# Where VectorE's sums stand in their slots, and seven products for every pair of token tiles from the fourth on

## The chip, the cores and the metric

The kernel runs on one core of a Trainium2 chip. The metric is the device time of one execution in microseconds (us); of the kernel before, 12 runs are at hand. One further execution was profiled, and all durations below are from it. The engines are called PE (TensorE's matmuls), PEld (its weight loads), DVE (VectorE), ACT (ScalarE), POOL (GpSimd) and SP (SyncE, which issues DMAs).

## What is computed

Attention with a sliding window of 128 and a bias that falls linearly with distance, for 8 batches of 576 tokens and 8 heads of 64, and behind it a two-layer block on all 4608 tokens:

```python
scores = scale * q @ k.T                       # per batch and head
mask = (rel >= 0) & (rel < 128)                # rel = query position - key position
attn = softmax(where(mask, scores - slope * |rel|, -1e9))
x = (attn @ v), heads side by side             # 4608 x 512
h = x @ w_in                                   # 4608 x 2048
g = where(h > 0, h, exp(min(h, 0)) - 1)        # ELU
out = g @ w_out                                # 4608 x 512, float32
```

## The kernel before, in words

The kernel's order is written out by hand. Its unit of order is the **slot**: slots 0 to 151, and most of them hold one *hidden step*, PE's work for one PSUM bank of h, 128 x 512. Tokens are cut into nine tiles t of 512, and for the output into 18 **pairs** n of 256 tokens (two tiles of 128 rows each). What a slot issues is set by lists that are filled beforehand and walked at L646 to L659, in this order: `early` (exponentials of attention scores), the hidden step (`hidden`, L292), the ELU's last operation of the step before (`done`, L523), `tasks` in the order in which they were entered, `OUT` (output matmuls), and `late`. Each engine works strictly through its own instructions in that order, so a place in the list is a place in every engine's queue.

**Hidden step and ELU.** PE fills one of the two banks hp[0] and hp[1] (L300), in turn. Then there are two ways. In a slot that the set SOFT names, ACT does a relu (L307) and an exponential (L308). In any other, ACT does one exponential (L310) and POOL a min and max (L311). Either way DVE follows with one scalar_tensor_tensor (L318) in the next slot, which writes g and frees the bank, so the hidden step two slots on waits for it.

**Attention.** For batches 2 to 7 each batch takes 17 slots from START[b] (L587), in four units of four slots. In a unit's first slot PE computes scores at the end (L225), into four banks. In its second and third slot ACT takes the exponentials (L231, four a unit, two at the head of each slot), and DVE multiplies by a table (`weigh`, L236, two a unit). In its fourth slot PE multiplies by v (`all_values`, L266), DVE divides (L271, L272: a reciprocal and a product, "the norm"), and SP turns the result into xT by a DMA. A short fifth step ends the batch (L248, L254, L255). DVE also turns q and k of a later batch (`turn_qk`, L145).

**Output.** Pairs outside the list SEVEN (L511), which are 0, 1, 2, 6 and 10, use plain products: 32 matmuls of 512 columns, four a slot (L324), and two copies by ACT (L331). The other 13 pairs use seven products in place of eight (Strassen's scheme in Winograd's form): 56 matmuls of 256 columns, seven a slot (L388), over eight slots from s = 15 + 8n. They need four sums of halves of g by DVE, S1 to S4 (`sums`, L358, each 128 x 1024 in float16), three sums of results, C11, C12, C22 (`combine`, L395, each 128 x 256 in float32), five copies by ACT (L391, L393), and differences of w_out that are made once, in eight halves, in slots 26 to 39 (`quarters`, L351). Call p = (s - 15) mod 8 the phase of a slot. S1 of a pair is made in the slot before its first (p = 7), S2 at p = 1, S3 at p = 3, S4 at p = 4. C11 is in `late` at p = 2, C12 in `late` at p = 6, C22 in the tasks of p = 0 of the next pair. The product that needs S2 begins with the third matmul of p = 2. The banks op and av change roles after each pair of SEVEN (XY, L513).

Because the attention tasks are entered into the lists first (L591 to L617), the sums of a slot stand behind its weights, norms and turns in DVE's queue.

Of the kernel before, what the change touches and what calls it, by code (L numbers as in the profile page):

```python
# [18 lines left out]
def kernel(  # L19
# [14 lines left out]
    NTB = NTOK // 512  # L34
# [114 lines left out]
    with tc.manual_schedule():  # L149
# [142 lines left out]
        def hidden(t, c0, w, f0, nf, p, soft):  # L292
            hps[t, c0, f0] = p
            a = (512 * t + c0) % RING
            cuts = [(0, w, a)] if a + w <= RING else [(0, RING - a, a), (RING - a, w, 0)]
            for l in range(nf):
                fc = f0 + l
                for u0, u1, x0 in cuts:
                    for c in range(4):
                        nc.tensor.matmul(  # L300
                            p[:, l * w + u0:l * w + u1], w_in_sb[:, c, fc * 128:(fc + 1) * 128],
                            xT[:, c, x0:x0 + u1 - u0], start=(c == 0), stop=(c == 3))
            e = es[t, c0, f0] = work.tile([128, 512], F32, name="e", tag="e", bufs=6)
            n = w * nf
            if soft:

                nc.scalar.activation(e[:, 0:n], p[:, 0:n], AF.Relu, scale=-1.0)  # L307
                nc.scalar.activation(e[:, 0:n], e[:, 0:n], AF.Exp, scale=-1.0)  # L308
                return
            nc.scalar.activation(e[:, 0:n], p[:, 0:n], AF.Exp)  # L310
            nc.gpsimd.tensor_scalar(out=e[:, 0:n], in0=e[:, 0:n], scalar1=1.0, scalar2=0.0,  # L311
                                    op0=ALU.min, op1=ALU.max)
# [173 lines left out]
        early, tasks, late, HID, OUT = {}, {}, {}, {}, {}  # L486

        def at(s, f, *a):
            tasks.setdefault(s, []).append((f, a))

        def after(s, f, *a):
            late.setdefault(s, []).append((f, a))

# [13 lines left out]
        for t in range(2, NTB):  # L507
            for j in range(16):
                step = (128 * (j // 4), 128, 4 * (j % 4), 4) if t < 4 else (256 * (j // 8), 256, 2 * (j % 8), 2)
                HID[16 * t + 6 + j] = [(t, *step, BUF[(j + 1) % 2])]  # L510
        SEVEN = (17, 3, 4, 5, 7, 8, 9, 11, 12, 13, 14, 15, 16)  # L511

        XY = {1: (op, av)}  # L513
        for n in range(2, 2 * NTB):
            XY[n] = XY[n - 1][::-1] if n - 1 in SEVEN else XY[n - 1]
        for o in range(16 * NTB):
            t, ts, f = o // 16, o // 4 % 4, o % 4
            if o // 8 in SEVEN:
                continue
            s = (9, 11, 13, 14)[o] if o < 4 else 11 + o if o < 13 else 2 * o - 1 if o < 16 else 15 + o  # L520
# [70 lines left out]
        for b in range(2, B):  # L591
            for u in range(4):
                a = START[b] + 4 * u
                after(a, scores, b, u)
                for g in range(4):
                    before(a + 1 + g // 2, expo, b, u, g)
                at(a + 1, weigh, b, u, 0)
                at(a + 2, weigh, b, u, 1)
                at(a + 3, all_values, b, u)
                at(a + 3, turn, b, u)  # L600
                if u == 3:
                    at(a + 4, values, b, 4, 0, sp[2])
                    at(a + 4, values, b, 4, 1, sp[3])
                    at(a + 4, turn, b, 4)
            a = START[b - 1] if b > 2 else 0
            for n in range(4):
                piece = (b, int(n < 2), n % 2)
                if b == 2:
                    m = 4 if n < 2 else 6
                    at(TURN[b][n], turn_qk, *piece, 0, m)  # L610
                    at(REST[n], turn_qk, *piece, m, R)
                else:
                    at(TURN[b][n] if b == 3 else a + 4 * n, turn_qk, *piece)
            for n in range(8):
                at(a - 8 + n if a else 16 + n // 2, load_qk, b, int(n < 4), n % 4)
            for n in range(5):
                at(a + 3 + n if a else 20 + n // 2, load_v, b, n)  # L617


        for m, a in enumerate((26, 30, 31, 32, 34, 35, 36, 39)):  # L620
            at(a, quarters, 1 + m // 2, m % 2)
        turns = [(i, j) for i in (1, 2, 6, 5, 7, 3, 4) for j in range(8)]
        for n in SEVEN:
            s = 15 + 8 * n
            if n < 2 * NTB - 1:
                for d, i in ((-1, 1), (1, 2), (3, 3), (4, 4)):
                    at(s + d, sums, n, i)
                after(s + 2, combine, n, "C11")
                after(s + 6, combine, n, "C12")
                at(s + 8, combine, n, "C22")  # L630
                for d in range(8):
                    OUT[s + d] = [(product, (n, i, j, j + 1)) for i, j in turns[7 * d:7 * d + 7]]
            else:
                at(s - 3, sums, n, 3)
                for i in (1, 2):
                    at(s - 2, sums, n, i, 0, 6)
                    at(s - 1, sums, n, i, 6, 8)
                at(s - 1, product, n, 1)
                OUT[s] = [(product, (n, 2)), (combine, (n, "C11")), (sums, (n, 4)), (product, (n, 6)), (product, (n, 5))]
                OUT[s + 1] = [(product, (n, 7)), (product, (n, 3)), (combine, (n, "C12")), (combine, (n, "C22")),  # L640
                              (product, (n, 4)), (last_out, (n,))]


        SOFT = {15 + 8 * n + d for n in SEVEN for d in (-1, 1, 2, 3, 4)} | {26, 30, 31, 32, 34, 35, 36, 39} | set(range(16 * NTB - 10, 16 * NTB + 8))

        slots = set(HID) | set(OUT) | set(tasks) | set(early)  # L646
        for s in range(min(slots), max(slots) + 1):
            for f, a in early.get(s, []):
                f(*a)
            for step in HID.get(s, []):  # L650
                hidden(*step, s in SOFT)
            if s - 1 in HID and s not in (1, 4, 5):
# [37 lines left out]
```

## Time and profile before

| | |
|---|---|
| median of 12 runs | 314.06 us (313.53 to 316.18) |
| the profiled execution's own time | 314.49 us |
| its span, first to last instruction | 312.7 us |
| PE busy | 303.3 us, 97% |
| PEld busy | 248.6 us, 79% |
| DVE busy | 246.2 us, 79%, 470 instructions |
| ACT busy | 226.4 us, 72%, 432 instructions |
| POOL busy | 123.3 us, 39%, 189 instructions |
| granted TensorE clock | 0.998 |

Busy time counts an instruction from its start to its end. On DVE and ACT a following instruction may start before the one ahead has ended (a scalar_tensor_tensor lasts 0.68 us, but the next starts 0.60 us after it), so the distance from start to start is what an instruction takes of its engine. PE's recorded ends are modelled, and its matmuls overlap. A lost moment of PE shows best as a gap in the weight loads or as a distance between starts that is longer than usual.

### The profile page before, as it was taken

Reading aid. Unit: us, or ns where it says so; the run is one execution under the profiler, and the core shown is the slowest. Engines: PE = TensorE matmul, PEld = TensorE weight load, DVE = VectorE, ACT = ScalarE, POOL = GpSimd, SP = SyncE. Lnnn points to the kernel's source line nnn. Section 1 sums busy time; section 2 is a strip of 40 time slices with the busy share of each in tenths; the row PEclk is TensorE's granted clock in tenths of the full one; section 3 lists DMA queues with packets and bytes.
Section 4 is the critical chain, followed back from the end, with each engine's and each line's share of the span. In section 5 each row is a group of like instructions: output and inputs, shape, how many; then the busy total and the mean of one; then the engine's idle time right before and its main releaser. Section 6 shows DMA issues by size and latency. Waiting matters only on the chain.

```text
span 312.7 us, 10087 instructions
## 1 busy us (share of the span) xinstructions
PE 303.3 (97%) x4231; PEld 248.6 (79%) x4231; DVE 246.2 (79%) x470; ACT 226.4 (72%) x432; POOL 123.3 (39%) x189
## 2 busy tenths in 40 slices
PE   6899999999999999999999999999999999999995
PEld 5688874786798888987788888777899778888884
DVE  5646656889889988886889898778898888886782
ACT  4576457688888677756887779647977787868871
POOL 8847879463333235263716071655210101010000
PEclk9999999999999999999999999999999999999999
DMA  9999999996893919898979999997921201130102
GB/s 97 179 198 201 201 179 151 148 114 68 84 147 67 143 17 146 62 163 93 101 62 141 106 108 73 159 128 64 92 79 27 78 19 55 48 94 1 69 36 101
DMA packets 96510, 32.05 MB, mean 102 GB/s; under 512 B 83920, under 2 KB 91984, under 8 KB 96464
## 3 DMA queue, kind: packets, MB, share of 16 engines
q0 software_dynamic: 75920, 18.36, 65.3%
q1 hardware_dynamic: 20400, 12.98, 18.0%
q8 instruction: 33, 0.54, 0.7%
q14 instruction: 13, 0.11, 0.1%
q10 hardware_dynamic: 144, 0.07, 0.1%
HBM read 36.70 MB, written 9.44 MB: 148 GB/s over the span
## 4 chain that ended last, share of the span: by engine, by line
PE 82%; DVE 6%; ACT 4%; issue 3%; DMA 2%; POOL 1%; DVEq 0%; POOLq 0%; ACTq 0%
PE hp L300 35%; PE op L388 10%; PE av L388 9%; PE op L324 6%; PE spa L225 4%; PE av L324 3%; ACT EX L231 3%; PE spa L266 3%; DVE g L318 2%; DMA s<-in_q_dram 2%; PE sp L388 1%; PE sp L248 1%; PE sp L324 1%; PE sp L300 1%; PE spa L176 1%
## 5 line engine op out<-in xcount | busy, mean ns | idle before, releaser
L300 PE MATMUL hp<-xT,wi 128*128 128x128 f16 (+2 forms) x1744 | 144.9, 233 | 2.1 <-DVE rden L254 0.6
L300 PEld LDWEIGHTS <-wi 128*128 128x128 f16 x1856 | 124.4, 98 | 22.4 <-issue 7.4
L318 DVE SCALAR_TENSOR_TENSOR g<-e,hp 128x512 f16<-128x512 f32 x138 | 94.1, 682 | 23.6 <-POOL e L311 16.2
L311 POOL TENSOR_SCALAR e<-e 128x512 f32<-128x512 f32 x70 | 43.9, 627 | 149.4 <-ACT e L310 148.7
L307 ACT ACTIVATE e<-hp 128x512 f32<-128x512 f32 x74 | 44.3, 599 | 25.1 <-PE hp L300 22.0
L310 ACT ACTIVATE e<-hp 128x512 f32<-128x512 f32 x64 | 38.5, 602 | 27.0 <-PE hp L300 24.5
L308 ACT ACTIVATE e<-e 128x512 f32<-128x512 f32 x74 | 46.7, 631 | 2.4
L236 DVE TENSOR_TENSOR EX<-EX,TAB 128x1024 f16<-128x1024 f16 x48 | 33.1, 690 | 15.4 <-ACT EX L231 15.1
L388 PEld LDWEIGHTS <-S 128*128 128x128 f16 x416 | 38.7, 98 | 6.7 <-DVE S L349 2.4
L114 POOL DMA_DIRECT2D VP<-in_v_dram x40 | 34.5, 870 | 2.0 <-PE sp L324 1.2
L231 ACT ACTIVATE EX<-spa 128x512 f16<-128x512 f32 x48 | 26.1, 596 | 8.0 <-PE spa L225 8.0
L388 PEld LDWEIGHTS <-g 128*128 128x128 f16 x312 | 29.2, 98 | 3.0
L231 ACT ACTIVATE EX<-sp 128x512 f16<-128x512 f32 x48 | 26.1, 601 | 0.0
L324 PE MATMUL op<-wo,g 128*128 128x512 f16 x96 | 24.7, 379 | 0.0
L324 PEld LDWEIGHTS <-g 128*128 128x128 f16 x160 | 13.7, 97 | 10.8 <-issue 1.1
L388 PE MATMUL op<-s,S 128*128 128x256 f16 x144 | 21.6, 273 | 0.5 <-DVE S L349 0.4
L388 PE MATMUL av<-s,S 128*128 128x256 f16 x144 | 21.6, 273 | 0.2 <-DVE S L349 0.2
L349 DVE TENSOR_TENSOR S<-g 128x1024 f16<-128x1024 f16 (+2 forms) x27 | 17.8, 660 | 0.3 <-PE av L388 0.2
L272 DVE TENSOR_TENSOR xn<-spa,rden 128x512 f16<-128x512 f32 x24 | 16.6, 691 | 0.8
L108 POOL DMA_DIRECT2D st<-in_k_dram x24 | 16.3, 685 | 0.0
L108 POOL DMA_DIRECT2D st<-in_q_dram x24 | 16.0, 672 | 0.0
L225 PE MATMUL sp<-QT,KT 32*128 32x256 f16 (+2 forms) x240 | 15.1, 250 | 0.0
(142 smaller groups left out, 389.4 us busy)
## 6 DMA issues: line engine op xcount, KB each, us to landing
out_dram<-ob SPq DMA_DIRECT2D x35, 256.0 KB, 3.0
VP<-in_v_dram POOLq DMA_DIRECT2D x32, 128.0 KB, 5.1
st<-in_k_dram POOLq DMA_DIRECT2D x24, 144.0 KB, 4.1
st<-in_q_dram POOLq DMA_DIRECT2D x24, 144.0 KB, 4.8
wi<-in_moe_w_in_dram POOLq DMA_DIRECT2D x4, 512.0 KB, 11.8
wo<-in_moe_w_out_dram POOLq DMA_DIRECT2D x4, 512.0 KB, 11.4
VP<-in_v_dram POOLq DMA_DIRECT2D x8, 64.0 KB, 5.5
s<-in_k_dram POOLq DMA_DIRECT2D x1, 512.0 KB, 13.3
```

Source lines behind the costliest of these rows:

```text
L108: nc.gpsimd.dma_start(st[b][32 * g:32 * g + 32, w, :, :, :, :].rearrange("p h n j d -> p (h n) (j d)"), (q, k)[w][b, 2 * g:2 * g + 2, :, : ...
L114: nc.gpsimd.dma_start(VP[b % 2][0:p, n, :, 0:D], v[b, :, 128 * n:128 * n + p, :].rearrange("h p d -> p h d"))
L231: nc.scalar.activation(unit(b, u)[:, g, :, :], sp[g].rearrange("p (h c) -> p h c", h=2), AF.Exp, scale=0.125)
L236: V.tensor_tensor(out=e, in0=e, in1=TAB[:, int(u == 3), 2 * gp:2 * gp + 2, :, :], op=ALU.mult)
L300: nc.tensor.matmul(p[:, l * w + u0:l * w + u1], w_in_sb[:, c, fc * 128:(fc + 1) * 128], xT[:, c, x0:x0 + u1 - u0], start=(c == 0), stop=(c ...
L307: nc.scalar.activation(e[:, 0:n], p[:, 0:n], AF.Relu, scale=-1.0)
L308: nc.scalar.activation(e[:, 0:n], e[:, 0:n], AF.Exp, scale=-1.0)
L310: nc.scalar.activation(e[:, 0:n], p[:, 0:n], AF.Exp)
L311: nc.gpsimd.tensor_scalar(out=e[:, 0:n], in0=e[:, 0:n], scalar1=1.0, scalar2=0.0, op0=ALU.min, op1=ALU.max)
L318: V.scalar_tensor_tensor(out=gs[t][:, f0:f0 + nf, c0:c0 + w], in0=sh(es.pop((t, c0, f0))), scalar=1.0, in1=sh(hps.pop((t, c0, f0))), op0=A ...
L324: nc.tensor.matmul(o, gs[t][:, fc, ts * 128:(ts + 1) * 128], w_out_sb[:, fc, :], start=(fc == 0), stop=(fc == NFC - 1))
L388: nc.tensor.matmul(o, a[:, j, :], b[:, j, :], start=j == 0 and i in (1, 2, 5), stop=j == 7, skip_group_check=True)
```

## The change

DVE's sums, C22 and the quarters are entered at the front of their slots' tasks by the new function `at_once`, so they stand right behind the scalar_tensor_tensor of the slot and ahead of weights, norms and turns. C11 and C12 stay in `late`. Of the last pair, the order of S1 and S2 in the code is swapped, because each is put in front of what is there; the resulting order is S1, S2 as before. Pairs 6 and 10 are done by seven products, so that all pairs from 3 to 17 are. And SOFT, which named the phases 7, 1, 2, 3, 4 of a pair of SEVEN, names 0 as well; with the two new pairs, 21 slots are new in it (47, 55, 63, ..., 127, eleven of phase 0, and 62, 64 to 67, 94, 96 to 99), and slot 38 is out.

```diff
+        def at_once(s, f, *a):
+            tasks.setdefault(s, []).insert(0, (f, a))
...
-        SEVEN = (17, 3, 4, 5, 7, 8, 9, 11, 12, 13, 14, 15, 16)
+        SEVEN = range(3, 18)
...
-            at(a, quarters, 1 + m // 2, m % 2)
+            at_once(a, quarters, 1 + m // 2, m % 2)
...
                 for d, i in ((-1, 1), (1, 2), (3, 3), (4, 4)):
-                    at(s + d, sums, n, i)
+                    at_once(s + d, sums, n, i)
                 after(s + 2, combine, n, "C11")
                 after(s + 6, combine, n, "C12")
-                at(s + 8, combine, n, "C22")
+                at_once(s + 8, combine, n, "C22")
...
-                at(s - 3, sums, n, 3)
-                for i in (1, 2):
-                    at(s - 2, sums, n, i, 0, 6)
-                    at(s - 1, sums, n, i, 6, 8)
+                at_once(s - 3, sums, n, 3)
+                for i in (2, 1):
+                    at_once(s - 2, sums, n, i, 0, 6)
+                    at_once(s - 1, sums, n, i, 6, 8)
...
-        SOFT = {15 + 8 * n + d for n in SEVEN for d in (-1, 1, 2, 3, 4)} | {26, 30, 31, 32, 34, 35, 36, 39} | set(range(16 * NTB - 10, 16 * NTB + 8))
+        SOFT = {15 + 8 * n + d for n in SEVEN for d in (0, 1, 2, 3, 4, 7)} | {26, 30, 31, 32, 34, 35, 36, 39} | set(range(16 * NTB - 10, 16 * NTB + 8))
```

## The prediction

> **What bounds the kernel now.** I read the page first, then who waited for whom, then the chain of work that ended last, and last the timeline of single slots.
>
> ```profile
> PE 303.3 (97%) x4231; PEld 248.6 (79%) x4231; DVE 246.2 (79%) x470; ACT 226.4 (72%) x432; POOL 123.3 (39%) x189
> ```
>
> PE carries the time: its matmuls follow each other almost without a gap, and 82% of the chain lies on it. So a change pays only by taking matmul time away or by ending one of PE's few stalls, and costs by adding stalls. Where are they? The waits:
>
> ```profile
> DVE EX L236 <- ACT EX L231: 15.1, 33, 0.9
> ...
> PEld L388 <- DVE S L349: 2.4, 6, 0.5
> ```
>
> Six times PE's loads stand 2.4 us in all for a sum S of DVE. A load would have waited one matmul's length (0.11 us) anyway, so PE itself loses 2.4 - 6 x 0.11 = 1.7 us (in slots 43, 49, 57, 91, 121 and 129). And DVE stands 15.1 us in front of its weights, waiting for ACT's exponentials, with the sums queued behind. The timeline of DVE, then of the weight loads, in slots 55 to 57 (batch 3) shows the worst place:
>
> ```profile
> 120.53 0.83 DVE L349 TENSOR_TENSOR ob<-U,U 128x256 f32<-128x256 f32 x1
> 121.29 0.68 DVE L318 SCALAR_TENSOR_TENSOR g<-e,hp 128x512 f16<-128x512 f32 x1
> 121.89 0.20 DVE L271 RECIPROCAL rden<-spa 128x8 f32<-128x8 f32 x1
> 122.12 0.69 DVE L272 TENSOR_TENSOR xn<-spa,rden 128x512 f16<-128x512 f32 x1
> 122.72 0.68 DVE L349 TENSOR_TENSOR S<-S,g 128x1024 f16<-128x1024 f16 x1
> ```
>
> ```profile
> 122.02 0.88 PEld L300 LDWEIGHTS <-wi 128*128 128x128 f16 x15 [0.28 <-issue]
> 122.85 0.15 PEld L388 LDWEIGHTS <-g 128*128 128x128 f16 x2
> 123.46 0.33 PEld L388 LDWEIGHTS <-S 128*128 128x128 f16 x4 [0.45 <-DVE S L349]
> ```
>
> Two stalls follow each other. At 122.02 the hidden step of slot 57 has stood 0.28 us: its bank is freed by the operation at 121.29, which came late because of the chain ACT, POOL and C22 (120.53, 0.83 us instead of its median of 0.42, beside a POOL operation of 120.47 to 121.09). At 123.46 the product that needs S2 has stood, because S2 (122.72) was behind the norm (122.12). The same pair of stalls comes in slots 121 (0.46 and 0.47) and 129 (0.32 and about 0.45).
>
> **The change, step by step.**
>
> *Sums in front.* No work is added for the old pairs. At 122.72 S2 would start right after 121.29's operation, at about 121.9, 0.8 us earlier, against a stall of 0.34. All six S stalls should end: **-1.7 us** (bounds -1.7 and -1.0, if the sum's own input is late). What is pushed back by one sum (0.60 to 0.67 us from start to start)? The weights: 33 of the 48 stand waiting for ACT, as this one of slot 59:
>
> ```profile
> 128.41 0.69 DVE L236 TENSOR_TENSOR EX<-EX,TAB 128x1024 f16<-128x1024 f16 x1 [0.56 <-ACT EX L231]
> ```
>
> For 0.56 us DVE idles in front of it. S4, which stands behind it now, fits there nearly whole, so the weight starts at the same moment, and values, which follow it without slack, are not delayed. Where that cover is missing (hard slots, where the exponentials come earlier) values have 0.3 to 0.7 us of slack behind the second weight; worst case 0.3 us each in four units. The norm goes back 0.6 us: the next scores, which need its bank, start 0.9 to 1.4 us after it now, so nothing waits. Behind it on SP's queue is the DMA that turns xn, also 0.6 us later; its tile is read six slots (12 us) later. C22 in front sends its output DMA ahead of that one. The quarters (slots 26 to 39) go ahead of norms that wait for PE's values anyway: 0, within 0.3 either way.
>
> *Phase 0 soft, C22 first.* A soft slot goes through ACT alone and takes POOL out. What it costs ACT, from starts of slot 76:
>
> ```profile
> 159.98 0.61 ACT L307 ACTIVATE e<-hp 128x512 f32<-128x512 f32 x1
> 160.62 0.63 ACT L308 ACTIVATE e<-e 128x512 f32<-128x512 f32 x1
> 161.16 0.35 ACT L391 COPY U<-op 128x256 f32<-128x256 f32 x1
> 161.41 1.09 ACT L231 ACTIVATE EX<-sp 128x512 f16<-128x512 f32 x2
> 162.38 0.61 ACT L310 ACTIVATE e<-hp 128x512 f32<-128x512 f32 x1
> ```
>
> Start to start: relu 0.64, exponential 0.54, so 1.18 against 0.47 for the single one (the next instruction starts at 162.85); a copy 0.25; two exponentials of scores 0.97. In slots 55, 119 and 127 the operation that frees the bank would start about 0.25 us earlier (exponential's end at 121.0, C22 already done) and POOL no longer stretches C22: the stalls of 0.28, 0.46 and 0.32 end, **-1.0 us** (bounds -1.06 and -0.3). Price elsewhere: where phase 0 is a unit's second slot (71, 79), its second pair of exponentials comes 0.7 us later, against 0.32 us of slack before its values: **+0.5 us** for both (0 to 1.2). The other stalls of that kind (slots 44, 48, 53, 61, 78, 125, 133; 1.4 us) wait at other phases, and I let them stay.
>
> *Pairs 6 and 10.* Here a rule of the Trainium skill speaks against the change. "TensorE: Matmul & The Clock Gate", section "Back-to-back issue gap", gives for a sustained stream of load and matmul about 81 ns at 128 columns and about 131 ns at 512. By it 32 plain matmuls are 4.2 us and 56 of 256 columns (between 81 and 131, say 98 ns, my estimate) 5.5 us: 1.3 us more per pair. The chain says otherwise, plain first, seven products below:
>
> ```profile
> 198.60 0.86 PE op L324 x4
> ...
> 276.90 0.76 PE av L388 x7
> ```
>
> 215 ns for 512 columns and 109 for 256: the trace decides. A slot's output work shrinks by 0.10 us, 16 slots by **1.6 us**, if PE still is the bound there. Now the other engines in these pairs, by windows (pairs 6, 7, 10, 11; columns are length, PE, PEld, DVE, ACT, POOL):
>
> ```profile
> 134.29:150.98 16.69, 16.69 (x227) 11.95 (x225) 13.12 (x25) 9.41 (x19) 9.22 (x14) 1.00 0.85 114
> 150.98:166.77 15.79, 15.78 (x204) 13.42 (x200) 13.03 (x23) 12.82 (x27) 6.89 (x10) 1.00 0.91 85
> 197.46:213.57 16.11, 16.11 (x178) 11.05 (x176) 11.65 (x22) 9.51 (x18) 8.67 (x14) 1.00 0.96 132
> 213.57:228.95 15.38, 15.38 (x186) 12.99 (x185) 13.69 (x25) 13.18 (x27) 6.04 (x8) 1.00 1.03 77
> ```
>
> Each gets four sums (2.5 us), three C (1.1), and on ACT five soft slots (3.6) and 0.3 net of copies: DVE 15 to 17 us of busy time, about 14 from start to start, and ACT 13.3, in about 16. On average it fits, but ACT's bursts are longer than the stretch beside them. So I take the time of slots of equal phase in pairs that are already so built. Slots 66 to 70 take 10.56 us now (140.42 to 150.98); slots 74 to 78, of the same place in unit and pair, with seven products, 10.41. Slots 95 to 98 take 8.01, their likes 87 to 90 take 7.71. For 62 to 65, counting ACT forward from 132.84 (two exponentials, soft, copy, two exponentials, soft) frees slot 65's bank at 138.3, against a start at 138.18 now: 0. For 99 to 102, which have scores as cover, 0.35. Sum -0.15 - 0 - 0.30 - 0.35 = **-0.8 us** (bounds -1.6 and +1.0, the latter if ACT's bursts cost 0.3 us in each of six units).
>
> Sum: -1.7 - 1.0 + 0.5 - 0.8 = -3.0; I give 0.2 back for the worst case of the weights, which is not zero: -2.8. The profiled execution's 314.49 (span 312.7 and 1.8 around it) becomes 311.7. It lies 0.43 above the median of the runs, so the median of the changed kernel should be **311.3 us**.
>
> **The rivals.**
>
> *A, likeliest, as above: 311.3, own range 309.8 to 312.6; chance 0.56.*
>
> *B, all of it.* The matmuls' 1.6 us come in full, half of the other 1.4 us of stalls goes, slots 71 and 79 cost nothing: -1.7 - 1.0 - 1.6 - 0.7 = -5.0, **309.1**. For it: DVE's 15.1 us of idling in front of weights. Against: in pairs 7 and 11, built so already, ACT is at 81 and 86%. Chance 0.14.
>
> *C, the waits move on.* The sums come in time, but the operation that frees the bank is what ends last, and the hidden step behind waits instead; pairs 6 and 10 give nothing. Of 1.7 + 1.0 only a quarter stays: -0.7, **313.4**. For it: at 122.02 and 123.46 both stalls lie within 1.5 us, DVE was busy throughout. Against: after it DVE idles again. Chance 0.15.
>
> *D, slower: ACT becomes the bound.* With p = 7, 0, 1, 2, 3, 4 there are six soft slots in a row. ACT needs 6 x 1.18 + 4 x 0.25 + two units' exponentials 4 x 0.97 = 12.0 us; PE takes about 11 us for such a stretch (slots 54 to 59: 11.7, less 0.6 of stalls). The lag of 0.9 us meets a slack of about 0.4 (from a hidden step's end to the step two on PE has 2.4 us, and the soft chain needs 2.0). 0.3 us of stall in each of 12 pairs is 3.6; slots 71 and 79 add 0.5, pairs 6 and 10 lose 0.5 more in place of a gain: +4.6, against -2.7 from the stalls that end: +1.9, **316.0**. It outweighs the gains from 0.14 us a pair on (12 x 0.14 + 0.5 + 0.5 = 2.7). Against: the hard slots at p = 5, 6 let ACT catch up, and the lag needs both units inside the stretch. Chance 0.15.
>
> **How the numbers follow.** A measurement of this kernel can tell 0.3%, 0.94 us, from no change, so faster is below 313.1 and slower above 315.0. A and B lie below (a twentieth of A above): 0.67, with a third of C (0.05): 0.72. The same: most of C, the rest of A, a little of D: 0.15. Slower: 0.13. The range, 309.0 to 315.0, leaves out half of B below and most of D above, 0.2 in all.
>
> **What would show it.** In the changed profile: no wait of PEld at L388 for S above 0.5 us in all; no gap before the first loads of slots 57, 121, 129; C22 at 0.42 us wherever POOL is idle; the idle time of DVE in front of L236 down by half; L324 in no slot after 38. ACT's busy time up by about 14 us (20 soft slots by 0.63, and the copies). Right on A if the stretch of slots 62 to 70 shortens by less than 0.4 us while 95 to 102 shortens by 0.5 or more. Wrong towards D if loads at L300 stand for an operation of DVE that waited for ACT's exponential at L308, in most pairs; wrong in the first step if L266's second half waits for L236, because a sum took the weight's place.

## The result

The changed kernel takes 312.1 us (median of 12 runs, 311.54 to 313.46), the kernel before 314.4 us over the runs that now are at hand (49). The ratio is 0.9932, with a 95% interval of 0.9915 to 0.995: faster by 0.7%, some 2.1 us. The forecast was 311.3 of 314.06, a ratio of 0.991, in a range of 309.0 to 315.0.

The profiled execution took 311.12 us, its span is 309.4 us, 3.3 less than before. Not all of that is the change. Slot 1's hidden step begins 1.0 us earlier in the profile of after, though nothing ahead of it was changed; and slot 0 alone differs by up to 0.4 us between profiles. From there on, slots that an edit doesn't touch agree between two profiles to a few ns, with few exceptions: slot 1 differs by up to 0.12 us, slots 93 and 94 by up to 0.18, and slot 103 once by 0.24, and no edit explains them. So the yardstick for everything below is the **main part**, from the first weight load of slot 1's hidden step to that of slot 148: 283.35 us before, 281.00 after, **-2.35 us**. And each slot's length, from first weight load to first weight load, can be compared with the same slot of another kernel.

The first line of the page after, and two of its waits (engine and line that waited, who ended it; us, times, longest):

```profile
PE 302.3 (98%) x4279; PEld 254.5 (82%) x4279; DVE 251.7 (81%) x484; ACT 238.2 (77%) x458; POOL 111.3 (36%) x169
```

```profile
DVE g L318 <- ACT e L308: 12.6, 32, 0.9
...
DVE EX L236 <- ACT EX L231: 5.9, 15, 0.6
```

The wait of PEld at L388 for S (2.4 us before) is gone from the list. DVE's idling in front of weights fell from 15.1 to 5.9 us, since the sums fill it, and part of it moved to the front of the scalar_tensor_tensor (6.2 us before, 12.6 after, and 10.6 with the order alone), where DVE now arrives before ACT's exponential. The place that the prediction showed, at slots 56 and 57, now reads so on DVE and on the weight loads:

```profile
120.13 0.69 DVE L318 SCALAR_TENSOR_TENSOR g<-e,hp 128x512 f16<-128x512 f32 x1 [0.46 <-ACT e L308]
120.74 0.68 DVE L349 TENSOR_TENSOR S<-S,g 128x1024 f16<-128x1024 f16 x1
...
121.58 0.69 DVE L272 TENSOR_TENSOR xn<-spa,rden 128x512 f16<-128x512 f32 x1
```

```profile
120.70 1.05 PEld L300 LDWEIGHTS <-wi 128*128 128x128 f16 x16
121.71 0.15 PEld L388 LDWEIGHTS <-g 128*128 128x128 f16 x2
121.88 0.54 PEld L388 LDWEIGHTS <-S 128*128 128x128 f16 x5
```

The sum stands directly behind the scalar_tensor_tensor, the norm behind it, and the loads for S follow the loads for g without a wait; the hidden step's 16 loads stand in one row. Slot 57 went from 3.04 to 2.49 us.

Where the 2.35 us came from, by slots that differ by more than 0.05 us:

| slots | what was there before | change, us |
|---|---|---|
| 43 and 44, 49, 57, 91, 121, 129 | waits for S, and bank stalls | -0.39, -0.21, -0.55, -0.15, -0.58, -0.56: sum -2.44 |
| 63 to 70 | pair 6 by plain products | -0.19 |
| 95 to 102 | pair 10 by plain products | -0.58 |
| 27 to 32 | a quarter now ahead of a norm | +0.39 |
| 39, 103, 111 | a sum now ahead of a second weight (and slot 38, ahead of 39, now hard) | +0.28, +0.18, +0.13: sum +0.58 |
| all others | | -0.1 |

### The profile page after: what moved, and what is told of

Read it like the earlier page. It is cut to its first block, busy times and chain, and to the rows that moved or that the text cites. A ratio compares the mean times of both kernels' runs of the same rounds, so it can differ in the third digit from the quotient of the medians.

```text
span 309.4 us, 10228 instructions
## 1 busy us (share of the span) xinstructions
PE 302.3 (98%) x4279; PEld 254.5 (82%) x4279; DVE 251.7 (81%) x484; ACT 238.2 (77%) x458; POOL 111.3 (36%) x169
## 4 chain that ended last, share of the span: by engine, by line
PE 69%; DVE 9%; issue 6%; ACT 5%; DMA 5%; POOL 4%; POOLq 0%; SPq 0%; DVEq 0%; ACTq 0%
PE hp L300 30%; PE op L388 11%; PE av L388 11%; DVE g L318 3%; PE spa L225 3%; PE op L324 3%; DMA wi<-in_moe_w_in_dram 3%; PE spa L266 2%; DMA out_dram<-ob 2%; POOL e L311 2%; ACT EX L231 2%; ACT e L310 2%; PE sp L388 1%; DVE EX L236 1%; PE sp L324 1%
## 5 line engine op out<-in xcount | busy, mean ns | idle before, releaser
L318 DVE SCALAR_TENSOR_TENSOR g<-e,hp 128x512 f16<-128x512 f32 x138 | 93.8, 679 | 25.9 <-ACT e L308 12.6
L311 POOL TENSOR_SCALAR e<-e 128x512 f32<-128x512 f32 x50 | 31.4, 628 | 159.0 <-ACT e L310 158.6
L308 ACT ACTIVATE e<-e 128x512 f32<-128x512 f32 x94 | 59.3, 631 | 3.0
L388 PEld LDWEIGHTS <-S 128*128 128x128 f16 x480 | 45.2, 98 | 4.9
L236 DVE TENSOR_TENSOR EX<-EX,TAB 128x1024 f16<-128x1024 f16 x48 | 33.4, 695 | 6.0 <-ACT EX L231 5.9
L388 PEld LDWEIGHTS <-g 128*128 128x128 f16 x360 | 33.7, 98 | 3.5
L388 PE MATMUL op<-s,S 128*128 128x256 f16 x168 | 25.2, 272 | 0.0
L388 PE MATMUL av<-s,S 128*128 128x256 f16 x168 | 25.2, 272 | 0.0
L349 DVE TENSOR_TENSOR S<-g 128x1024 f16<-128x1024 f16 (+2 forms) x31 | 20.8, 670 | 0.8 <-PE av L388 0.2
L388 PE MATMUL av<-wo,g 128*128 128x256 f16 x112 | 16.8, 272 | 0.0
L388 PE MATMUL op<-wo,g 128*128 128x256 f16 x112 | 16.8, 273 | 0.0
L324 PE MATMUL op<-wo,g 128*128 128x512 f16 x64 | 16.4, 379 | 0.0
```

Of the source, the lines that this page charges most:

```text
L236: V.tensor_tensor(out=e, in0=e, in1=TAB[:, int(u == 3), 2 * gp:2 * gp + 2, :, :], op=ALU.mult)
L318: V.scalar_tensor_tensor(out=gs[t][:, f0:f0 + nf, c0:c0 + w], in0=sh(es.pop((t, c0, f0))), scalar=1.0, in1=sh(hps.pop((t, c0, f0))), op0=A ...
L324: nc.tensor.matmul(o, gs[t][:, fc, ts * 128:(ts + 1) * 128], w_out_sb[:, fc, :], start=(fc == 0), stop=(fc == NFC - 1))
L388: nc.tensor.matmul(o, a[:, j, :], b[:, j, :], start=j == 0 and i in (1, 2, 5), stop=j == 7, skip_group_check=True)
```

## The experiments

Each is told by its edit, against the kernel before, the whole change or, once, another experiment, by its main part, and by the slots that moved. Where no ratio stands, the kernel was timed once, with its profile, and the slots alone decide.

**The order alone** (the whole change with SEVEN and the phases of SOFT as before).

```diff
-        SEVEN = range(3, 18)
+        SEVEN = (17, 3, 4, 5, 7, 8, 9, 11, 12, 13, 14, 15, 16)
-        ... for d in (0, 1, 2, 3, 4, 7)} ...
+        ... for d in (-1, 1, 2, 3, 4)} ...
```

> Main part means the time from the first weight load of slot 0's hidden step to that of slot 148: 284.95 us before, 282.60 with the whole change (-2.35). This kernel has the order alone: sums, C22 and quarters in front; the list of pairs and the soft slots as before. My theory (the order ends the waits for S and costs where a weight or a norm is pushed behind a sum): six S stalls end, -1.7, of the bank stalls at p = 2 a part, -0.3, and +0.7 at slots 27, 31, 39, +0.1 at 111: -1.2 in the main part, time ratio 0.996. Rival M (the gain is the matmul time of the two pairs): 0 to +0.5. Rival P (the soft slots of phase 0 ended the stalls, not the order): -0.3 or less gain.

Measured: 0.9954 (0.9938 to 0.997); main part -1.38. Slots 43 and 44, 49, 57, 91, 121, 129 shortened by 0.40, 0.22, 0.50, 0.25, 0.52, 0.52, in sum 2.4 us: all that the whole change wins there, bank stalls included, though at slots 57, 121 and 129 it takes 0.15 us off each bank stall, and the whole change 0.20. It lost 0.38 at slots 27 to 32, 0.13 at 47, 0.10 at 73, 0.29 at 81, 0.16 at 90, 0.10 at 111. Slot 39 lost nothing: slot 38 is soft here. Rivals M and P fall.

**The pairs alone** (SEVEN with 6 and 10 put in, all else as before).

```diff
-        SEVEN = (17, 3, 4, 5, 7, 8, 9, 11, 12, 13, 14, 15, 16)
+        SEVEN = (17, 3, 4, 5, 6, 7, 8, 9, 10, 11, 12, 13, 14, 15, 16)
```

> Pairs 6 and 10 by seven products with soft slots at p = 7, 1, 2, 3, 4 as the other pairs had; order and phase 0 as before. My theory (in these pairs ACT's bursts eat most of the 1.6 us of matmul time): -0.5 in the main part, within 0.4. Rival M: -1.6. Rival P says nothing here.

Measured: 0.9989 (0.9973 to 1.0004), no change that can be told; main part -0.61. Seven slots of the pairs lost 0.10 us each, as the matmuls give it; slot 65 gained 0.16 and slot 70 0.08 in return.

**Phase 0 alone.**

```diff
-        ... for d in (-1, 1, 2, 3, 4)} ...
+        ... for d in (-1, 0, 1, 2, 3, 4)} ...
```

> The slots of phase 0 soft, all else as before. My theory: the S stalls stay (1.7 us), the bank stalls of slots 57, 121, 129 shrink by some 0.6 in all, slots 71 to 81 lose 0.2: -0.4 in the main part. Rival P: -1.7 to -2.4, the S waits vanish too. Rival M: 0.

Measured: 0.9987 (0.9971 to 1.0004); main part -0.57: slots 57, 121 and 129 by 0.20 each, and the waits of PEld for S stay at 2.4 us, 6 times. These 0.20 are bank stall, for the first weight load of the slot is followed that much sooner by the second. So a soft phase 0 takes a part of the bank stalls when the order is old, as the theory had it, and none of the waits for S. With six soft slots in a row now in most pairs, slots 71 to 81 lost nothing in sum.

**The quarters back behind the norms**, all else as in the whole change.

```diff
-            at_once(a, quarters, 1 + m // 2, m % 2)
+            at(a, quarters, 1 + m // 2, m % 2)
```

> The whole change, with the eight quarters again behind the norms of slots 26 to 39. My theory: the 0.22 at slot 27 and the 0.26 at slot 31 go, the 0.28 at slot 39 (a sum ahead of a weight) stays: -0.4 against the whole change, main part 282.2. Rivals M and P: no change.

Measured: 0.9935 (0.9917 to 0.9953). The two medians can't be told apart, but the slots can: 27 by -0.23, 31 by -0.26, 29 and 32 by +0.09, in sum -0.39 as expected, and slot 39 as in the whole change. The main part is 280.46, 0.55 less than with the whole change; the other 0.16 are slots that the quarters don't touch, slot 1 above all. What slot 27 waited for stands in the whole change's timeline, DVE's norm and the loads of the transposes behind it:

```profile
61.57 0.42 DVE L255 TENSOR_TENSOR xn<-av,rden 128x256 f16<-128x256 f32 x1
...
62.05 0.17 PEld L284 LDWEIGHTS <-xn 128*128 128x128 f16 x3 [0.22 <-DVE xn L255]
```

With the quarter behind it the norm starts 0.6 us earlier, and the four loads go through without a gap.

**The whole change without the two pairs.**

```diff
-        SEVEN = range(3, 18)
+        SEVEN = (17, 3, 4, 5, 7, 8, 9, 11, 12, 13, 14, 15, 16)
```

> From here on the main part is counted from the first weight load of slot 1's hidden step to that of slot 148, since slot 0 alone differs by up to 0.4 us between profiles: 283.35 us before, 281.00 with the whole change, -1.38 with the order alone, -0.61 with the pairs alone, -0.57 with phase 0 alone. This kernel is the whole change with pairs 6 and 10 by plain products. If the parts add up, -1.95. If the pairs gain more once the sums stand in front (rival M), -1.4 or less gain; if they only work against ACT's load, -2.2.

Measured: main part -1.56, 0.79 less gain than the whole change. But this edit does more than its name says: with the old SEVEN and the new phases, slots 70 and 102 are hard, which are soft in both kernels. Slot 103 pays for it: the weight in slot 102 takes 1.10 us there, and slot 103 is 0.26 us longer than with the whole change. So the total fits none of the three forecasts cleanly, and single slots have to be read.

In the pairs' own slots, 63 to 70 and 95 to 102, this kernel agrees with the one before to a few ns, and the whole change is 0.76 us shorter. With the pairs alone these slots gave 0.46. So rival M, as put here, holds in part: the new order makes the pairs worth 0.3 us more, at slots 65 (0.20) and 100 (0.18), against 0.07 lost at slot 70. At slots 57, 121 and 129 the order alone gave 1.53, phase 0 alone 0.60, and both together 1.70: most of the bank stall that one ends, the other ends as well.

**The slots of the two pairs hard.**

```diff
-        SOFT = {15 + 8 * n + d for n in SEVEN for d in (0, 1, 2, 3, 4, 7)} | ...
+        SOFT = {15 + 8 * n + d for n in SEVEN if n not in (6, 10) for d in (0, 1, 2, 3, 4, 7)} | ...
```

> The whole change with slots 63 to 67, 70, 95 to 99 and 102 through POOL (hard). My theory (ACT's bursts from these soft slots cost the stalls of slots 65, 66, 69, 70, 99, 0.7 us in all): stall of 0.36 at slot 70 gone, 0.4 to 0.7 faster than the whole change. Rival N (DVE's added sums are what makes PE stand): no faster, and stalls at other slots of the same pairs, because POOL beside the sums is slower.

Measured: main part 281.75, 0.75 *slower* than the whole change. Slot 70's stall did go (-0.35), but slot 66 is longer by 0.49, 69 by 0.33, 98 by 0.23, 103 by 0.35 (slot 102 is hard here too). The pairs' own slots alone are 0.69 longer. The timeline of slot 65 and the start of 66:

```profile
137.38 1.18 DVE L349 TENSOR_TENSOR S<-S,g 128x1024 f16<-128x1024 f16 x1
137.39 0.62 POOL L311 TENSOR_SCALAR e<-e 128x512 f32<-128x512 f32 x1
...
140.06 0.32 PEld L300 LDWEIGHTS <-wi 128*128 128x128 f16 x5 [0.41 <-issue]
```

S2 starts in the same moment as POOL's min and max and takes 1.18 us in place of 0.68. All that DVE does behind it is late by half a microsecond, and slot 66's hidden step stands 0.41. My theory of ACT's bursts falls as the whole of the matter; rival N holds.

**The ten soft slots, with plain products** (the kernel before, so ACT has the load and DVE no sum).

```diff
+        SOFT = ... | {62, 64, 65, 66, 67, 94, 96, 97, 98, 99} | ...
```

> The kernel before, with the ten slots 62, 64 to 67, 94, 96 to 99 soft and pairs 6 and 10 still by plain products, so ACT has the soft slots without any sum. My theory: 0.3 to 0.6 slower than before, at slots 65 to 70. Rival N: 0.

Measured: main part +0.002 us. Of the pairs' slots only 65 is longer, by 0.07; the other nine soft slots of ACT cost nothing. A second blow to that theory.

**Weights first where DVE doesn't wait for them**: the quarters behind the norms, and three of the sums S1 behind the weights.

```diff
-            at_once(a, quarters, 1 + m // 2, m % 2)
+            at(a, quarters, 1 + m // 2, m % 2)
-                    at_once(s + d, sums, n, i)
+                    (at if i == 1 and n in (3, 11, 12) else at_once)(s + d, sums, n, i)
```

> The whole change, but quarters behind the norms, and S1 of pairs 3, 11 and 12 (slots 38, 102, 110, where a unit's second weight is due and its exponentials are already there) behind the weights. My theory (a sum in front costs where DVE does not stand waiting for ACT): the 0.43 of slots 27 to 32 and 0.28, 0.17, 0.13 of slots 39, 103, 111 go: 1.0 faster than the whole change, time ratio to before 0.990. If the sum is late for its product then, S waits come back at slots 39, 103, 111, and the gain is 0.4 alone.

Measured: 0.9872 (0.9845 to 0.9899), 310.64 us against 314.36, the fastest of all, and clear of the whole change's interval; main part 279.84, 1.16 less than with the whole change: slots 27 to 32 by 0.39 in sum, 39 by 0.27, 103 by 0.28, 111 by 0.13, and 0.1 elsewhere. How slot 39 looked with the whole change (timeline of slots 38 and 39):

```profile
84.12 0.69 DVE L349 TENSOR_TENSOR S<-g 128x1024 f16<-128x1024 f16 x1
84.52 0.77 POOL L311 TENSOR_SCALAR e<-e 128x512 f32<-128x512 f32 x1 [0.30 <-ACT e L310]
84.73 1.10 DVE L236 TENSOR_TENSOR EX<-EX,TAB 128x1024 f16<-128x1024 f16 x1
...
85.88 0.29 PEld L266 LDWEIGHTS <-EX 128*128 128x128 f16 x8 [0.22 <-DVE EX L236]
```

and with the weight first, on DVE and on the weight loads:

```profile
83.98 0.68 DVE L236 TENSOR_TENSOR EX<-EX,TAB 128x1024 f16<-128x1024 f16 x1
84.58 1.10 DVE L349 TENSOR_TENSOR S<-g 128x1024 f16<-128x1024 f16 x1
```

```profile
85.30 0.58 PEld L266 LDWEIGHTS <-EX 128*128 128x128 f16 x16
```

Two things had met in slot 38. The weight had gone behind the sum, though its exponentials were done 1.1 us before it began (ACT's last ended at 83.64). And it had met POOL's operation, since slot 38 is now hard: 1.10 us in place of 0.69. The order alone, with slot 38 soft, lost nothing at slot 39, so the first without the second is free here. The 16 loads for values, in two halves with a gap before, now go through in one row. The sum takes the 1.10 us instead, and nobody waits for it.

**Phase 0 hard, with the rest of the change.**

```diff
-        ... for d in (0, 1, 2, 3, 4, 7)} ...
+        ... for d in (1, 2, 3, 4, 7)} ...
```

> The whole change with the phase 0 slots hard again (47, 55, ..., 127). If phase 0 adds to the order what it gave alone, the main part from slot 1 is 0.6 longer than with the whole change, at slots 57, 121, 129. If the order had already ended those stalls (C22 in front comes before POOL's operation), 0.2 or less there, and what is lost is lost at slots 73 and 81, where S2 now stands in front of the second weight.

Measured: main part 281.67, 0.67 longer than with the whole change, but only 0.05 of it at each of slots 57, 121 and 129; slots 73 and 81 lost 0.38 each. (In the profiles of this and the next two kernels the granted clock fell to between 0.5 and 0.8 in the second of the 40 slices, ahead of slot 1; in all slices behind it stood at 0.9 or more.) Slots 72 and 73:

```profile
153.00 0.68 DVE L236 TENSOR_TENSOR EX<-EX,TAB 128x1024 f16<-128x1024 f16 x1
153.21 0.95 POOL L311 TENSOR_SCALAR e<-e 128x512 f32<-128x512 f32 x1 [2.28 <-ACT e L310]
...
154.19 0.69 DVE L318 SCALAR_TENSOR_TENSOR g<-e,hp 128x512 f16<-128x512 f32 x1 [0.51 <-POOL e L311]
...
154.93 0.75 PEld L300 LDWEIGHTS <-wi 128*128 128x128 f16 x7 [0.31 <-issue]
```

C22 in front pushed the first weight to 153.00, beside POOL's operation, which then took 0.95 us in place of 0.61. The scalar_tensor_tensor waits for it, and the hidden step for that. Here it is POOL that is held up by DVE.

**Slot 67 hard**, against the kernel with the weights first.

```diff
+        SOFT -= {67}
```

> The kernel with the weights first, and slot 67 hard. ACT then has 0.7 us less to do in front of the exponential of slot 68. My theory (slot 70 stands 0.36 us for ACT's burst in unit 66): that stall goes, 0.2 to 0.35 faster than with the weights first. Rival N (DVE and POOL stand in each other's way): the stall moves to slot 69, because POOL's operation meets the weight or S4, and nothing is gained.

Measured: slot 70 by -0.35, slot 69 by +0.35. The whole main part differs by +0.08 (slot 103 +0.24, others -0.15). At slot 103 POOL's operation of slot 101 began 0.3 us later behind its exponential than in the other kernel; why, isn't shown. The stall of slot 70 is ACT's, as its chain in the whole change shows:

```profile
144.79 0.61 ACT L310 ACTIVATE e<-hp 128x512 f32<-128x512 f32 x1
...
145.56 0.62 POOL L311 TENSOR_SCALAR e<-e 128x512 f32<-128x512 f32 x1 [11.07 <-ACT e L310]
...
146.21 0.69 DVE L318 SCALAR_TENSOR_TENSOR g<-e,hp 128x512 f16<-128x512 f32 x1 [0.57 <-POOL e L311]
...
146.96 0.75 PEld L300 LDWEIGHTS <-wi 128*128 128x128 f16 x7 [0.37 <-issue]
```

The exponential of slot 68 starts when ACT is through with unit 66's, and POOL, DVE and PE follow one after the other. With slot 67 hard ACT is early enough, but slot 69 then reads:

```profile
145.51 1.15 POOL L311 TENSOR_SCALAR e<-e 128x512 f32<-128x512 f32 x1 [8.59 <-ACT e L310]
...
147.44 0.88 PEld L300 LDWEIGHTS <-wi 128*128 128x128 f16 x15 [0.45 <-issue]
```

POOL's operation begins with the first weight (also at 145.51) and takes 1.15 us. The same 0.35 us are lost one slot earlier.

**POOL beside the sums, by itself.** In the soft slots of the last two tiles two operations of POOL were added whose result nobody reads; nothing that the output needs was changed.

```diff
                 nc.scalar.activation(e[:, 0:n], e[:, 0:n], AF.Exp, scale=-1.0)
+                if t > 6:
+                    for _ in range(2):
+                        nc.gpsimd.tensor_scalar(out=idle[:, 0:n], in0=e[:, 0:n], scalar1=1.0, scalar2=0.0,
+                                                op0=ALU.min, op1=ALU.max)
                 return
```

> The whole change, and in the soft slots of the last two token tiles (slots 118 to 149) two operations of POOL on e after ACT's exponential, written to a tile that nobody reads: the same min and max that a hard slot has. The second overlaps the sum that follows. Rival N (a two-input operation of DVE in SBUF and an operation of POOL exclude each other): sums, weights or C22 in these slots take 1.0 to 1.2 us in place of 0.68 (0.8 in place of 0.42), or POOL's operations 1.2 in place of 0.62, in many places; slots before 118 stay as they are. If not: durations within 5%.

Measured: main part +0.48, of which slots 120 to 135 take all (slots 124 and 132 +0.36 each); before slot 118 nothing moved beyond slot 0. On DVE in slots 122 and 123 (its lines are five higher here):

```profile
252.12 0.69 DVE L354 TENSOR_TENSOR S<-g 128x1024 f16<-128x1024 f16 x1
252.73 1.09 DVE L236 TENSOR_TENSOR EX<-EX,TAB 128x1024 f16<-128x1024 f16 x1
```

Two added operations of POOL lie beside this sum and weight (251.65 to 253.28); the first took 0.61 us, the second 0.93. In the whole trace 14 of POOL's operations took 0.9 us or more, four weights in these slots 1.06 to 1.10 and two more 0.79, against 0.69. The sums, the operations it was meant for, took 0.76 at most but for one of 0.85 in the last slots, and one C22 took 0.62 in place of 0.42: mostly POOL gave way to the sum and then held the weight. No scalar_tensor_tensor, which reads one input from PSUM, took more than 0.69, though 35 of them overlapped an operation of POOL by more than 0.1 us.

## Why the prediction was right, and where it wasn't

*Sums in front, -1.7: right, in size and in cause.* The six places gave -2.44 with the whole change. Of it 0.66 is shorter bank stalls; the other 1.8 are the waits for S, and the order alone ended them.

*Bank stalls, -1.0: the cause was right, the size was not.* Counted as what stands between the first two weight loads of the hidden step beyond the usual 0.11 us, the stalls of slots 57, 121 and 129 fell from 0.27, 0.44 and 0.31 us to 0.07, 0.24 and 0.11: 0.6 in all. The prediction let the operation that frees the bank start 0.25 us earlier and yet let stalls of 0.46 and 0.32 end wholly, which its own number doesn't give. What is left waits for the exponential of the soft slot. Slot 121 after, DVE and the second of its eight loads:

```profile
246.12 0.69 DVE L318 SCALAR_TENSOR_TENSOR g<-e,hp 128x512 f16<-128x512 f32 x1 [0.46 <-ACT e L308]
...
246.86 0.75 PEld L300 LDWEIGHTS <-wi 128*128 128x128 f16 x7 [0.25 <-issue]
```

The prediction gave the gain to the soft phase 0 and C22 in front together. Either alone does most of it (phase 0 0.20 us a slot, the order 0.15), and with both it is 0.20. Either way C22 no longer meets POOL's operation: before, five of the 13 took 0.83 us; with phase 0 alone none took over 0.42, with the order alone one took 0.72, and after none of the 15 took over 0.42.

*Phase 0, +0.5 at slots 71 and 79: wrong.* The second exponentials come later, but values weren't held up, and with POOL the price would have been 0.38 at each of slots 73 and 81. The term should have been a gain (0.67 us in the new order). The step took the slack of values behind the second weight, and left out what POOL's operation does beside a weight.

*What is pushed back: too small.* Quarters were put at 0 within 0.3, weights at 0.2: measured +0.39 and +0.58. This is where the prediction failed by most. It named the condition (no cover where exponentials come early) and bounded it by 0.3 us each in four units; three came, with 0.28, 0.18 and 0.13, the first only because slot 38 had also become hard. Its own sign of an error in the first step, that L266's second half waits for L236, stands in the profile after at two places, 0.5 us in all. The quarters had been said to stand before norms that wait for PE. In slots 27 and 31 the transposes of PE waited for such a norm.

*Pairs 6 and 10, -0.8: the size was right (-0.76 in their own slots), the reason only in part.* The way of sizing, by slots of equal phase in pairs already so built, came out: -0.13, -0.06, -0.30 and -0.28 for slots 62 to 65, 66 to 70, 95 to 98 and 99 to 102, where 0, -0.15, -0.30 and -0.35 were forecast. The matmuls gave 0.1 us a slot as the trace of before had them, not the loss that the prediction had worked out from the Trainium skill's sustained figures ("TensorE: Matmul & The Clock Gate", section "Back-to-back issue gap"). What eats the rest was put to ACT's bursts. ACT's load alone costs next to nothing (soft slots with plain products: 0.07 at slot 65), and taking it away makes the pairs slower (by 0.69). It is true for one place, slot 70 (0.36 us). That 62 to 70 would shorten by less than 0.4 us and 95 to 102 by 0.5 or more came out: 0.19 and 0.58. The windows of the two pairs after (length, PE, PEld, DVE, ACT, POOL) show DVE and ACT where the prediction had them:

```profile
132.74:149.25 16.51, 16.32 (x251) 14.34 (x249) 14.24 (x28) 13.14 (x28) 5.20 (x8) 1.00 0.73 95
195.67:211.21 15.54, 15.54 (x202) 13.37 (x200) 14.24 (x28) 13.28 (x27) 5.77 (x9) 1.00 1.07 119
```

*The total.* The terms had -2.8, the main part gave -2.35. Of the terms 0.3 too much was taken for the waits, 0.8 too little for what is pushed back, and 0.5 of price at phase 0 that didn't come, with 0.1 of small gains. That the total came so near is in part luck: errors of 1.1 us one way and 0.6 the other make up for each other.

*The rivals.* C (the waits move on) falls: the operation that frees the bank wasn't late behind the sum. D (ACT becomes the bound) falls by phase 0 alone, which puts six soft slots in a row and still gains 0.57, and by the whole change, where the same slots hard cost 0.67; DVE does wait for ACT's exponential more often, but the loads of the hidden steps stand idle for 6.4 us in 27 places where before it was 7.4 us in 31. B's matmul gain of 1.6 us didn't come in full. Of pair 6's missing 0.6 us, 0.36 is slot 70. A stall of 0.07 us at slot 65 stands there with soft slots and plain products too; those of slots 66 and 69 (0.08 and 0.10) stay open.

## What to carry to other kernels

Put work that another engine waits for into the place where its own engine stands idle, waiting for a third engine: here DVE's idling in front of the weights was the cover for the sums. But ask it for each place; where the input of the next instruction is already there, the same move pushes it back by the whole length of what was put in front, which cost 0.13 to 0.28 us a slot here. And when an operation is moved on one engine, look at what then runs beside it on the other engines, here POOL, not only at what stands behind it in its own queue.

## What the runs showed of the hardware

DVE's tensor_tensor with both inputs in SBUF and POOL's tensor_scalar hold each other up when they run side by side: a sum of 0.68 us took 1.18, weights of 0.69 took 1.10, C22 of 0.42 took 0.83, and POOL's operation of 0.61 took up to 1.25. One or the other pays, by up to about the time the other needs; a scalar_tensor_tensor with one input in PSUM pays nothing. The Trainium skill has the rule ("SBUF — State Buffer", section "Who interferes with whom"): DVE with two inputs in SBUF and a GpSimd instruction that reads SBUF contend for a read interface that they share, and the order of issue decides who is blocked. The runs agree that the two contend, and that now DVE and now POOL is the late one. The order they don't settle: in the kernel with the pairs' slots hard, the sum that began at 137.38, 0.01 us ahead of POOL, was the one that paid, and POOL's operation at 141.83, 0.10 us ahead of a sum, took 1.25 us. The prediction had the 0.83 us of C22 before its eyes and took it as a matter of that one place; what the runs add is that it sets the price of each slot that goes through POOL near a sum or a weight.
